# A third exponential tile added on GpSimd in quads 5 to 21 of an attention kernel

## The chip, the cores and the metric

The kernel runs on one NeuronCore of a Trainium2 chip. The metric is the device time of one execution in microseconds, as the median of several runs. TensorE is called PE here, VectorE DVE, ScalarE ACT, GpSimd POOL, and SyncE, which issues most of the DMAs, SP. All data is fp32.

## The reference

The program is an attention with normalised queries and keys, followed by a feed-forward block with the SoLU activation.

```python
# 8 batches, 12 heads, 448 tokens, head size 64
q_n, k_n = rmsnorm(q, g_q), rmsnorm(k, g_k)
scores = q_n @ k_n.T / sqrt(64)
attn = exp(scores - max(scores)); attn = attn / (sum(attn) + 1e-9)
x = (attn @ v), heads side by side             # 3584 tokens x 768
h = x @ w_in                                   # 768 x 1024
solu = h * softmax(h)
y = layernorm(solu) * g_ln @ w_out             # 1024 x 768
```

The part that matters here is the sum of the exponentials over the keys, by which each query's output is divided.

## The kernel before

**Stages.** The attention comes first, then the first product of the feed-forward block (L989), then the second (L1203). Both products are cut into blocks that are combined by sums and differences so that fewer matmuls are needed; POOL makes the combinations of the weights (`combine`, L563). The whole attention lies in one hand-written order of instructions: each engine gets its instructions in the order in which the Python code calls them, and runs them in that order.

**Quads.** The loop at L1383 runs over 24 quads `m`. A quad is four heads, handled as two pairs: `a = 2m` and `b = 2m + 1`. A pair's state is the dictionary `st[n]`, a quad's is `quads[m]`.

**Exponentials.** The 448 keys of a head are three tiles of 128 and a rest of 64. `scores(n, kc)` (L810) multiplies one key tile with all the queries of the pair's two heads into a score tile in PSUM, of which there are three in rotation (`ps_t`, tag `t`), and ACT writes the exponentials to SBUF as `E[n, kc]`, 128 keys by 896 (two heads of 448 queries). The two rests of a quad share one more tile, `E[NJ]` (`scores_last`, L824). No maximum is taken off. The E tiles come from eight rotating buffers.

**Values.** `values_last` and `values` (L852, L865) multiply the tiles with v on PE into the PSUM tiles `o`. Every E tile is read there.

**Sums.** The sum over keys is a sum over partitions, and PE makes it with columns of ones: `sums(m)` (L876) accumulates several terms in the PSUM tile `sm`. Each term is one 128x896 tile and takes four matmuls, each of 224 columns and 32 rows of output (L890). To save terms, DVE first adds the first two tiles of each pair to one, `es` (`add`, L842). Quads 0 to 21 then have five terms: the shared tile of rests, the third tile of a, the third tile of b, es of a and es of b. In the last two quads (`on_vector`, L839) DVE also adds the third tile to es (`add_more`, L847), and there are three terms. Es has two buffers.

**After the sums.** `inverse` (L895) transposes `sm` on DVE (L901), takes the reciprocal (L902) and copies parts of it on POOL (L909). `divide` (L911), called one unit later, spreads the reciprocals (L916) and multiplies (L917); `store_x` (L920) writes the result to DRAM.

**Work for later quads in the same loop.** In quad m the queries and keys of quad m+2 are squared on ACT (`squares`, L662), summed by rows on DVE (`row_sums`, L670), and folded on POOL (`fold_sums`, four copies at L680 and an addition at L681). At the start of the next quad ACT makes the seed of the inverse root from that (L700, L701), DVE refines it (L707 to L710), and POOL multiplies queries and keys by it (`normalise`, L719). DVE transposes the result (`qk_transpose`, L729), ACT applies the gain (`gain`, L733). One raw tile of w_in is converted over two quads in each of quads 4 to 10 and in every second quad after that: two steps on ACT (L535, L536), and in the following quad two joins on DVE (L541, L542).

**Order in a quad from 5 on.** On POOL: `normalise` of a+2 and b+2, combinations of weights in some quads, the fold for quad m+2, the copies of `inverse`. On DVE: the refinement, the division of quad m-1, two transposes, `add(a)`, row sums of a+4 and of b+4, `add(b)`, joins, then `inverse`. On ACT: the seed, seven exponentials, two squares, two gains, conversion steps. On PE: seven score tiles, `values_last` and `values(a)`, `values(b)`, `sums`. The order around the change is at L1482 to L1515:

```python
            unit(lambda: scores(b, 1))
            if early or 1 < m < 4:
                qk_transpose(b + 2)
            if m > 1:
                add(a)
            unit(lambda: scores(b, 2))
            ...
            add_more(a)
            add_more(b)
            unit(outputs)
```

Of the kernel before, what the change touches and what calls it, by code (L numbers as in the profile page):

```python
# [14 lines left out]
OP = AluOpType  # L15
# [351 lines left out]
def fast_path(  # L367
# [24 lines left out]
    nc = tc.nc  # L392
# [225 lines left out]
    st = {}  # L618
# [187 lines left out]
    def exponentials(d, kc, s):  # L806
        d["E", kc] = big_tile("E")[:, 0 : 2 * S].rearrange("p (h t) -> p h t", h=2)
        nc.scalar.activation(d["E", kc], s[:, :, 0:S], AF.Exp)  # L808

    def scores(n, kc):  # L810
        d = st[n]
        s = ps_t.tile([P, 2, 512], FP32, tag="t", name="s")

        for c in range(0, P, D):
            for h in range(2):
                hh = slice(h * D, (h + 1) * D)
                keys = slice(NJ * c + kc, NJ * (c + D - 1) + kc + 1, NJ)
                nc.tensor.matmul(  # L818
                    s[c : c + D, h, 0:S], d["qkT"][hh, 1, keys], d["qkT"][hh, 0, :],
                    start=True, stop=True,  # L820
                )
        exponentials(d, kc, s)
# [16 lines left out]
    def on_vector(m):  # L839
        return m >= NQ - 2  # L840

    def add(n):  # L842
        d = st[n]
        d["es"] = work.tile([P, 2, S], FP32, tag="es", name="es")
        nc.vector.tensor_tensor(d["es"], d["E", 0], d["E", 1], OP.add)  # L845

    def add_more(n):  # L847
        d = st[n]
        if on_vector(n // 2):
            nc.vector.tensor_tensor(d["es"], d["es"], d["E", 2], OP.add)  # L850

    def values_last(m):  # L852

# [22 lines left out]
    def sums(m):  # L876


        d = quads[m]
        sm = d["sm"] = ps_t.tile([P, S // 2], FP32, tag="t", name="sm")  # L880
        terms = [(2, d["E", NJ])]
        for key in ("es",) if on_vector(m) else (2, "es"):
            for i in range(2):
                n = st[2 * m + i]
                terms.append((i, n["E", 2] if key == 2 else n["es"]))
        for x, (w, e) in enumerate(terms):
            for h in range(2):
                for t in range(2):
                    g = 32 * (2 * h + t)
                    nc.tensor.matmul(  # L890
                        sm[g : g + 32, :], ones[:, w], e[:, h, t * S // 2 : (t + 1) * S // 2],
                        start=(x == 0), stop=(x == len(terms) - 1),
                    )
# [421 lines left out]
    def unit(f, steps=4):  # L1315
        nonlocal now
        f()
        now += steps
        due = [x for x in todo if x[0] <= now]
        todo[:] = [x for x in todo if x[0] > now]  # L1320
        for _, g in sorted(due, key=lambda x: x[0]):
            g()
# [40 lines left out]
    with tc.manual_schedule():  # L1363
# [19 lines left out]
        for m in range(NQ):  # L1383
            a, b = 2 * m, 2 * m + 1
# [9 lines left out]
            if m == 0:  # L1394
# [32 lines left out]
                unit(lambda: values(b))  # L1427
                squares(5)
                unit(lambda: sums(m))
                inverse(m)  # L1430
                row_sums(4)
# [52 lines left out]
                qk_transpose(b + 2)  # L1484
            if m > 1:
                add(a)
            unit(lambda: scores(b, 2))
            if m == 1:
                qk_transpose(a + 2)
# [19 lines left out]
                fold_sums(m + 2)  # L1509
            if not scarce:  # L1510
                add(b)
            add_more(a)
            add_more(b)
            unit(outputs)
            step(m - 2)  # L1515
            begin(m)
# [7 lines left out]
            if m == NQ - 1:  # L1524
                block_sums(0, 0)
                block_sums(0, 1)
                load_x(1)
            unit(lambda: sums(m))
            inverse(m)
            if next1 and m not in (1, 2):  # L1530
# [139 lines left out]
@with_exitstack  # L1670
def kernel(
    ctx: ExitStack,
    tc: tile.TileContext,
    q: bass.AP,
    k: bass.AP,
    v: bass.AP,
    g_q: bass.AP,
    g_k: bass.AP,
    moe_w_in: bass.AP,
    moe_w_out: bass.AP,  # L1680
    moe_g_ln: bass.AP,
    out: bass.AP,
):
    nc = tc.nc
    flags = ctx.enter_context(tc.tile_pool(name="flags", bufs=1))
    flag = flags.tile([1, 1], I32, name="flag")
    large = flags.tile([1, 1], FP32, name="large")
    fast_path(tc, q, k, v, moe_w_in, moe_w_out, out, g_q, g_k, moe_g_ln, large)
    nc.vector.tensor_copy(flag, large)
    other = nc.values_load(flag[0:1, 0:1], min_val=0, max_val=1)  # L1690
    with tc.If(other > 0):
        general_path(tc, q, k, v, g_q, g_k, moe_w_in, moe_w_out, moe_g_ln, out)
# [30 lines left out]
```

## Time and profile before

| | |
|---|---|
| median of 3 runs | 816.29 us (816.02 to 816.68) |
| profiled execution | 815.47 us |
| its span | 813.7 us |
| mean granted PE clock | 0.998 of full speed |
| PE busy | 797.9 us |
| DVE busy | 617.0 us |
| ACT busy | 473.9 us |
| POOL busy | 469.0 us |

The attention fills the time to about 325.5 us, where the first matmul of the feed-forward block starts. In a row of the groups, `x` is the number of instructions, then come the busy time in us and the mean of one in ns, then the idle time of the engine just before them and what ended it. In a timeline a row gives the start and the length in us, the engine, the line and the operation, output and input tiles with their shapes, and in brackets the idle time before it and what ended that. Rows with a count stand for several instructions in a row. In a chain a row gives start, length and the line that the end of the span is traced back to. An fp32 matmul leaves two records, so a count of records on PE is twice the number of matmuls.

### The profile page before, as it was taken

To read this page: it belongs to the slowest core of one execution; us is meant where nothing else is said; L and a number is where in the kernel's file an instruction comes from. 1 tells how busy PE (TensorE), PEld (TensorE's weight loads), DVE (VectorE), ACT (ScalarE), POOL (GpSimd) and SP (SyncE) were. 2 spreads that over 40 slices of the span, in tenths; PEclk is the share of its full clock that TensorE was granted. 3 is DMA by queue.
4 is the path that set the end of the run, shared out by engine and by line. 5 is a ranking of instruction groups with operands and counts; after the bars stand their busy time and mean duration, and the time that the engine had idled before them with its cause. 6 is when DMAs were issued, how large, how long until landed. Compare 5 with 4: busy or idle time off the path is not lost.

```text
span 813.7 us, 14586 instructions
## 1 busy us (share of the span) xinstructions
PE 797.9 (98%) x5030; PEld 468.4 (58%) x5030; DVE 617.0 (76%) x1217; ACT 473.9 (58%) x785; POOL 469.0 (58%) x635
## 2 busy tenths in 40 slices
PE   8999999999999999999999999999989999999997
PEld 4334444444444443444444444444679999999996
DVE  6877889888887977478878756777796876866945
ACT  6677878777786865365767545444515454464420
POOL 1353555656555566233356467767497867777761
PEclk9999999999999999999999999999999999999999
DMA  9868798887878644245755344552548457365412
GB/s 165 175 143 157 165 184 185 188 178 159 163 162 180 132 94 123 81 131 142 184 142 146 91 113 122 147 137 64 171 122 279 129 197 245 122 239 181 150 60 83
DMA packets 269600, 122.71 MB, mean 151 GB/s; under 512 B 187596, under 2 KB 254668, under 8 KB 269516
## 3 DMA queue, kind: packets, MB, share of 16 engines
q1 hardware_dynamic: 254332, 111.78, 55.1%
q10 hardware_dynamic: 15184, 9.90, 4.5%
q8 instruction: 42, 0.69, 0.4%
q14 instruction: 42, 0.34, 0.1%
HBM read 84.94 MB, written 36.70 MB: 149 GB/s over the span
## 4 chain that ended last, share of the span: by engine, by line
PE 88%; DVE 5%; POOL 2%; DMA 2%; ACT 2%; issue 1%; SPq 0%; DVEq 0%; POOLq 0%; ACTq 0%
PE A L1203 14%; PE A L989 13%; PE o L871 13%; PE s L818 12%; PE B L989 8%; PE B L1203 7%; PE sm L890 5%; PE C L989 4%; PE D L989 4%; PE C L1203 3%; PE o L860 2%; PE s L831 2%; DMA xg<-xd 1%; ACT E L808 1%; DVE bs L1072 1%
## 5 line engine op out<-in xcount | busy, mean ns | idle before, releaser
L808 ACT ACTIVATE E<-s 128x896 f32<-128x896 f32 x168 | 139.1, 937 | 20.3 <-PE s L818 20.0
L818 PE MATMUL s<-qkT 64*64 64x448 f32 x1152 | 120.5, 545 | 1.4 <-ACT E L808 0.7
L871 PE MATMUL o<-E,v 128*64 128x448 f32 x576 | 113.5, 543 | 0.0
L680 POOL COPY ss<-part 32x56 f32<-32x56 f32 x88 | 42.1, 478 | 91.5 <-DVE part L670 88.8
L719 POOL TENSOR_TENSOR qkn<-qk,ny 128x896 f32<-128x896 f32 x46 | 77.1, 1697 | 21.2 <-DMA qk<-in_k_dram 12.0
L1078 POOL TENSOR_TENSOR he<-he,mhalf 128x1 f32<-128x1 f32 x28 | 27.6, 986 | 105.6 <-DVE he L1077 105.1
L1203 PE MATMUL B<-w_out,sums 128*128 128x192 f32 x392 | 80.0, 327 | 3.3 <-DVE P L1265 2.1
L818 PEld LDWEIGHTS s<-qkT 64*64 64x64 f32 x1152 | 48.1, 163 | 59.6 <-ACT E L808 29.2
L1203 PE MATMUL A<-w_out,sums 128*128 128x192 f32 x392 | 80.0, 327 | 1.2 <-POOL sums L1183 0.8
L871 PEld LDWEIGHTS o<-E,v 128*64 128x64 f32 x576 | 39.2, 137 | 72.7 <-issue 67.3
L989 PE MATMUL B<-w_in,xsum 128*128 128x512 f32 x168 | 76.7, 592 | 0.7 <-POOL he L1078 0.7
L989 PE MATMUL A<-w_in,xg 128*128 128x512 f32 x168 | 74.6, 593 | 0.0
L1060 ACT ACTIVATE u<-h,hmax 128x1024 f32<-128x1024 f32 x28 | 32.2, 1148 | 63.4 <-DVE hmax L1054 63.3
L1203 PEld LDWEIGHTS B<-w_out,sums 128*128 128x128 f32 x392 | 66.1, 190 | 4.0 <-DVE P L1265 2.4
L1203 PEld LDWEIGHTS A<-w_out,sums 128*128 128x128 f32 x392 | 66.1, 190 | 2.1 <-POOL sums L1183 1.3
L989 PEld LDWEIGHTS B<-w_in,xsum 128*128 128x128 f32 x168 | 31.8, 190 | 41.2 <-issue 38.3
L989 PEld LDWEIGHTS A<-w_in,xg 128*128 128x128 f32 x168 | 31.8, 190 | 40.1 <-issue 39.6
L845 DVE TENSOR_TENSOR es<-E 128x896 f32<-128x896 f32 x48 | 53.4, 1114 | 1.3 <-ACT E L808 1.3
L670 DVE TENSOR_REDUCE part<-sq 128x28 f32<-128x896 f32 x46 | 48.1, 1078 | 2.4
L729 DVE STREAM_TRANSPOSE qkT<-qkn 128x896 f32<-128x896 f32 x46 | 48.5, 1088 | 1.8 <-POOL qkn L719 1.8
L1203 PE MATMUL A<-w_out,s 128*128 128x192 f32 x224 | 45.5, 326 | 0.0
L563 POOL TENSOR_TENSOR w_out<-w_out 128x384 f32<-128x384 f32 x44 | 44.5, 1017 | 1.3
(151 smaller groups left out, 1622.4 us busy)
## 6 DMA issues: line engine op xcount, KB each, us to landing
ur<-ud SPq DMA_DIRECT2D x60, 256.0 KB, 4.5
ud<-ub SPq DMA_DIRECT2D x112, 128.0 KB, 2.3
xd<-xo SPq DMA_DIRECT2D x48, 224.0 KB, 3.1
qk<-in_q_dram SPq DMA_DIRECT2D x92, 112.0 KB, 3.1
qk<-in_k_dram SPq DMA_DIRECT2D x92, 112.0 KB, 3.0
v<-in_v_dram SPq DMA_DIRECT2D x24, 384.0 KB, 4.4
out_dram<-P SPq DMA_DIRECT2D x19, 384.0 KB, 3.7
raw<-in_moe_w_in_dram SPq DMA_DIRECT2D x12, 512.0 KB, 4.7
```

Of the source, the lines that this page charges most:

```text
L563: nc.gpsimd.tensor_tensor(o, p, q, OP.subtract)
L670: nc.vector.tensor_reduce(norms[m]["part"][:, i], st[n]["sq"], AX, OP.add)
L680: e.tensor_copy(ss[g * 32 : g * 32 + 32], part[o * 32 : o * 32 + 32])
L719: e.tensor_tensor(d["qkn"].rearrange("p (s b) d -> p s b d", s=2), d["qk"].rearrange("p s (b d) -> p s b d", d=32), y.rearrange("p (s b) - ...
L729: nc.vector.transpose(d["qkT"].rearrange("p s t -> p (s t)"), d["qkn"].rearrange("p b d -> p (b d)"))
L808: nc.scalar.activation(d["E", kc], s[:, :, 0:S], AF.Exp)
L818: nc.tensor.matmul(s[c : c + D, h, 0:S], d["qkT"][hh, 1, keys], d["qkT"][hh, 0, :], start=True, stop=True,)
L845: nc.vector.tensor_tensor(d["es"], d["E", 0], d["E", 1], OP.add)
L871: nc.tensor.matmul(d["o"][h * D : (h + 1) * D, :], quads[n // 2]["v"][:, n % 2 + 2 * h, kc], d["E", kc][:, h], start=False, stop=(kc == NJ ...
L890: nc.tensor.matmul(sm[g : g + 32, :], ones[:, w], e[:, h, t * S // 2 : (t + 1) * S // 2], start=(x == 0), stop=(x == len(terms) - 1),)
L989: nc.tensor.matmul(k[bank], a[:, c], w_in[i][:, c], start=begin and c == 0, stop=c == HD - 1, skip_group_check=not begin,)
L1203: nc.tensor.matmul(k[bank], a[:, c].rearrange("p a i -> p (a i)"), w_out[:, area, i, c], start=begin and c == 0, stop=c == KC - 1, skip_gr ...
```

## The change

In quads 5 to 21 the third tile of pair a is added to its es on POOL, right behind DVE's `add(a)` in the order of the code and ahead of the fold on POOL. The sums of these quads lose the term of that tile and have four terms. The third tile of pair b stays a term of its own. Quads 0 to 4 and the last two are as before; in the last two the two additions of `add_more` stay on DVE at their place.

```diff
+    def whole(n):
+        return on_vector(n // 2) or n > 9 and n % 2 < 1
+
     def add_more(n):
         d = st[n]
-        if on_vector(n // 2):
-            nc.vector.tensor_tensor(d["es"], d["es"], d["E", 2], OP.add)
+        if whole(n):
+            e = nc.vector if on_vector(n // 2) else nc.gpsimd
+            e.tensor_tensor(d["es"], d["es"], d["E", 2], OP.add)
...
         terms = [(2, d["E", NJ])]
-        for key in ("es",) if on_vector(m) else (2, "es"):
+        for key in (2, "es"):
             for i in range(2):
-                n = st[2 * m + i]
-                terms.append((i, n["E", 2] if key == 2 else n["es"]))
+                n = 2 * m + i
+                if key == "es":
+                    terms.append((i, st[n]["es"]))
+                elif not whole(n):
+                    terms.append((i, st[n]["E", 2]))
...
             if m > 1:
                 add(a)
+                if not on_vector(m):
+                    add_more(a)
             unit(lambda: scores(b, 2))
...
-            add_more(a)
-            add_more(b)
+            if on_vector(m):
+                add_more(a)
+                add_more(b)
             unit(outputs)
```

## The prediction

> **What bounds the kernel now.** I read the page first (busy shares, chain), then the chain by time inside the attention stage, then the timeline of each engine in one quad.
>
> ```profile
> span 813.7 us, 14586 instructions
> PE 797.9 (98%) x5030; PEld 468.4 (58%) x5030; DVE 617.0 (76%) x1217; ACT 473.9 (58%) x785; POOL 469.0 (58%) x635
> ```
>
> PE is busy for 98% of the span. The chain that ended last, cut to 95 to 130 us, is PE alone:
>
> ```profile
> 104.85 2.03 PE sm L890 x40
> 106.88 2.45 PE s L818 x24
> 109.33 0.75 PE s L831 x8
> 110.08 2.25 PE s L818 x24
> 112.34 0.75 PE o L860 x8
> 113.09 4.66 PE o L871 x24
> 117.75 2.03 PE sm L890 x40
> 119.78 2.45 PE s L818 x24
> ```
>
> A quad takes 119.78 - 106.88 = 12.90 us, and quads 5 to 21 all start that far apart, so PE sets the pace and the sums are 2.03 us of it. Each matmul has two records: 40 are 20 matmuls, five terms of four. From the timelines of quad 7, in the order POOL, DVE, ACT:
>
> ```profile
> 116.74 2.58 POOL L680 COPY ss<-part 32x56 f32<-32x56 f32 x4 [4.57 <-DVE part L670]
> 119.40 0.30 POOL L681 TENSOR_TENSOR ss<-ss,part 128x56 f32<-128x56 f32 x1
> 113.36 1.05 DVE L845 TENSOR_TENSOR es<-E 128x896 f32<-128x896 f32 x1
> 114.53 2.08 DVE L670 TENSOR_REDUCE part<-sq 128x28 f32<-128x896 f32 x2
> 116.53 1.08 DVE L845 TENSOR_TENSOR es<-E 128x896 f32<-128x896 f32 x1
> 119.84 0.42 DVE L901 STREAM_TRANSPOSE r<-sm 128x224 f32<-128x224 f32 x1 [0.88 <-PE sm L890]
> 119.74 0.34 ACT L700 ACTIVATE ny<-ss,eps 128x56 f32<-128x56 f32 x1 [1.97 <-POOL ss L681]
> 120.12 0.25 ACT L701 ACTIVATE ny<-ny 128x56 f32<-128x56 f32 x1
> 120.79 5.77 ACT L808 ACTIVATE E<-s 128x896 f32<-128x896 f32 x7 [0.42 <-PE s L818]
> ```
>
> What to see: POOL idles 4.57 us before the four copies, DVE waits 0.88 us for the sums, and ACT waits only 0.42 us for the first score tile. That 0.42 us is how far a second loop is from being the bound. This loop runs from seven exponentials through two squares on ACT, two row sums on DVE, the fold on POOL and the inverse root on ACT to the next exponentials. It is 12.90 - 0.42 = 12.48 us, some 12.52 with the 0.04 us by which an engine follows its releaser.
>
> **What the Trainium skill says.** "SBUF — State Buffer", section "Who interferes with whom": a DVE instruction with two SBUF inputs contends with a GpSimd instruction that reads SBUF, the first to issue holds the shared pair for the whole instruction, and a tensor_reduce never contends. The trace agrees. The four copies take 1.02 us where DVE runs neither an add nor a weight join, 1.75 beside the add es, and 2.58 beside it and the joins of L541 and L542:
>
> ```profile
> 79.05 1.02 POOL L680 COPY ss<-part 32x56 f32<-32x56 f32 x4 [5.57 <-DVE part L670]
> 181.22 1.75 POOL L680 COPY ss<-part 32x56 f32<-32x56 f32 x4 [4.56 <-DVE part L670]
> ```
>
> "Perfetto Trace Analysis", section "Optimizing Scalar/DVE Operations", warns that moving work between DVE and GpSimd might not help because of this port; here the work moves from PE, but the port still matters. Of the third page I use a price, below.
>
> **The change part by part.**
>
> *Removed from PE.* One term in each of quads 5 to 21, four matmuls (8 records). A quad with five terms spends 2.03 us in the sums. Quad 23, which already has three, spends 1.27 (324.26 to 325.53 in the chain). So a term is (2.03 - 1.27) / 2 = 0.38 us, and 17 x 0.38 = 6.46 us of PE time goes. The period PE asks for becomes 12.52 us.
>
> *Added on POOL.* 17 additions of 128x896 with two full inputs, written in place. No row shows it. Nearest rows:
>
> ```profile
> L563 POOL TENSOR_TENSOR w_out<-w_out 128x384 f32<-128x384 f32 x44 | 44.5, 1017 | 1.3
> L563 POOL TENSOR_TENSOR w_in<-w_in,w_in x12: 1272/1280/2045, 137.9 to 315.9; 128x512 f32<-128x512 f32 x12
> ```
>
> From 384 to 512 elements is 263 ns, 2.05 ns each, so 1280 + 384 x 2.05 = 2068 ns. "GPSIMD Engine Reference", section 3.1, gives 4497 ns for 2048 elements; scaled to 896 that is an estimate of 1967 plus some fixed cost, in agreement. Lower bound: the same-sized multiply of L719, 1697 ns, whose second input is a broadcast. Upper bound: 834 ns for 256 elements (L1181) without a fixed part, 2919 ns. I take 2.07 us.
>
> *When it runs.* It waits for es of a, which ends at 114.41 in quad 7. POOL follows DVE by 0.13 us (part ends 116.61, copies start 116.74), so it runs from 114.54 to 116.61, inside the 4.57 us of idleness. Beside it DVE runs the two row sums, which read one input and don't block it. Next on POOL are the fold's copies, held by part until 116.74; with the 0.08 us between POOL instructions they could start at 116.69. They aren't late. If the cover were gone, 2.07 us would go into the second loop each time.
>
> *The port.* DVE issues es of b at 116.53, with 0.08 us of the POOL addition left, and is blocked until 116.61. A blocked add finishes sooner after its release than its full duration: the one issued at 319.43 took 1.56 us but ended 0.95 after L970 let go at 320.04. So es of b ends near 117.6 as now, and joins and copies behind it keep their places. I put 0 to 0.1 us here.
>
> *The added waits.* Behind the waiting addition on POOL stands only the fold; ACT's inverse root waits for that. The combination of weights (L563, quads 9 to 21 in part) is ahead of it and ends before es of a does (139.21 against 140.19 in quad 9). PE now waits for POOL in the es term of a, which it reaches about 118.5, 1.9 us after the addition. Es has two buffers, as before, and E of a's third tile is still read by the values product, so no buffer is held longer. No DMA is added or moved; SP's queue is unchanged.
>
> *The second loop.* 12.52 us in the twelve quads with a weight join (5 to 11, 13, 15, 17, 19, 21), against PE's new 12.52: level. In the other five it has 2.58 - 1.75 = 0.83 us to spare, which also takes up what the quad before was late. PE feels lateness of ACT only when it lacks a score buffer, after about 0.1 to 0.2 us. So only the run of quads 5 to 11 can pile it up. At 0.05 us a quad that is 0.35 less about 0.15, so 0.2 us.
>
> *After quad 21* the stall at load xg (landing 312.65, ACT then late for quad 23) hangs on sums of 21 through divide and store, so it moves with them: 0.05 us for its own waits.
>
> Sum: 6.46 - 0.2 - 0.05 = 6.2 us. The profiled execution was 815.47 us (span 813.7, 1.8 around it); it becomes 809.3, span 807.5. The median of the runs is 816.29, 0.8 above that execution; minus 6.2 it is 810.1.
>
> **The rivals.**
>
> *Partly eaten by the second loop (811.9).* The addition takes 2.3 us, or the port's handover costs 0.2 to 0.3 us, so the twelve join quads are late by x = 0.25 us. Quads 5 to 11 lose 7 x 0.25 = 1.75; 13 to 21 lose 5 x (0.25 - 0.2) = 0.25, since each is followed by a quad with room. Gain 6.4 - 2.0 = 4.4 us. For it: the loop is level with PE to 0.05 us. Against it: the fit of 2.07, and a DVE that blocks nothing before es of b. Its spread, x from 0.1 to 0.4, is a gain of 5.6 to 2.5.
>
> *All of it eaten (816).* x near 0.6: 7 x 0.6 + 5 x 0.4 = 6.2, nothing left. This needs an addition of some 2.7 us, or copies that lose the port once more to a join (0.7 us).
>
> *Slower (818.5).* The GpSimd addition is the bound: at the upper price of 2.92 us it ends 0.80 us after the copies should start, and es of b, joins, copies and inverse root all follow it. Join quads 5 to 11 then take 12.52 + 0.80 = 13.32 us, 0.42 more than now, together +3.0. Quads 12 to 21 gain 10 x 0.38 = 3.8 and lose 5 x 0.6 = 3.0. Net +2.2 us. It decides from about 2.7 us on (x = 0.62 is break-even). Against it: only the short 256-element rows are that dear per element.
>
> That the change doesn't do what it says can't be: the removed term is in the instruction count, 136 fewer PE records.
>
> **How the numbers follow.** Full gain (5.6 to 6.5 us) 0.62; partly eaten (2.5 to 5.6) 0.22; eaten to within 0.2% (1.6 us, what a measurement of this kernel can tell from no change) 0.08; slower 0.08. PE caps the gain at 6.5 us, so the low end, with spread of the median, is 809.2; leaving out eaten and slower, the high end is 813.8. Faster 0.84, same 0.08, slower 0.08.
>
> **What would show it.** Sums at 1.65 us a quad with 32 records; starts of quads 5 to 21 12.52 us apart; a GpSimd row of 17 at about 2.07 us; ACT's wait for the first score tile down from 0.42 to near 0 in join quads; POOL's idle time before the copies from 4.57 to about 2.2, and copies still 2.58 and 1.75. Wrong if join quads are over 12.7 us apart, if es of b gets longer than 1.3 us, or if PE waits for ACT in the scores.

## The result and the profile after

The changed kernel takes 809.82 us (median of 4 runs, 809.46 to 811.44) against 816.15 us before. The ratio is 0.9928, with a 95% interval of 0.9911 to 0.9945. A later series of the same kernel, `after_again` below, gave 809.00 us and 0.9918 (0.9904 to 0.9932). The prediction was 810.1 us, between 809.2 and 813.8, and 807.5 us for the span of the profiled execution, which is 807.7 us. The later series lies just under the low end.

The first lines of the page of the changed kernel:

```profile
span 807.7 us, 14348 instructions
PE 793.2 (98%) x4894; PEld 466.1 (58%) x4894; DVE 615.4 (76%) x1217; ACT 474.0 (59%) x785; POOL 505.7 (63%) x652
```

PE has 136 records fewer (17 terms of 8), POOL has 17 instructions more and 36.7 us more work, and DVE and ACT have as many instructions as before. In the chain of the changed kernel the sums of quads 5 and 6 stand at:

```profile
87.43 4.66 PE o L875 x24
92.09 1.65 PE sm L897 x32
...
99.95 4.66 PE o L875 x24
104.61 1.65 PE sm L897 x32
```

The sums are 1.65 us long in place of 2.03, and the quads are 104.61 - 92.09 = 12.52 us apart in place of 12.90. The timelines of quad 7 of the changed kernel, in the order POOL, DVE, ACT:

```profile
113.93 2.11 POOL L854 TENSOR_TENSOR es<-es,E 128x896 f32<-128x896 f32 x1 [2.37 <-ACT sq L662]
116.12 2.58 POOL L680 COPY ss<-part 32x56 f32<-32x56 f32 x4
112.74 1.05 DVE L845 TENSOR_TENSOR es<-E 128x896 f32<-128x896 f32 x1
113.91 2.08 DVE L670 TENSOR_REDUCE part<-sq 128x28 f32<-128x896 f32 x2
115.91 1.08 DVE L845 TENSOR_TENSOR es<-E 128x896 f32<-128x896 f32 x1
118.84 0.42 DVE L908 STREAM_TRANSPOSE r<-sm 128x224 f32<-128x224 f32 x1 [0.49 <-PE sm L897]
119.50 0.25 ACT L701 ACTIVATE ny<-ny 128x56 f32<-128x56 f32 x1
119.79 5.77 ACT L808 ACTIVATE E<-s 128x896 f32<-128x896 f32 x7
```

The addition starts 0.14 us after es of a ends (113.79) and ends at 116.04. (The bracket names ACT's square, which ends at about the same time. By the order of the code the addition needs es and nothing of the square.) The fold's copies start at 116.12, 0.13 us after the row sums end at 115.99, the same distance as in the kernel before, so they start no later than the row sums let them. They also follow the addition by 0.08 us, the distance between two instructions on POOL seen before (119.32 to 119.40), so the addition fits with nothing to spare. Es of b takes 1.08 us as before, and the copies 2.58. DVE's wait for the sums is down from 0.88 to 0.49 us, and ACT no longer shows a wait at the first exponential.

Where the 6.0 us of the span came from, from the starts of `values_last` on PE (L860 before, L864 after) and the first matmul of the feed-forward block:

| | before | after | gain |
|---|---|---|---|
| quads 5 to 21, each | 12.89 to 12.90 us | 12.51 to 12.52 us | 17 x 0.379 = 6.44 |
| quad 22 to 23 | 13.06 us | 12.29 us | 0.77 |
| start of the kernel to quad 1 | 32.19 us | 32.32 us | -0.13 |
| all that follows the attention | 488.24 us | 489.31 us | -1.07 |

The first row is the change. The other three weren't expected. The start of quad 1 lies between 32.03 and 32.41 us in the ten traces of this case, so its 0.13 us is within what varies from one to another; the last section says more of the other two.

### The profile page after: what moved, and what is told of

It is laid out like the page before. It is cut to its first block, busy times and chain, and to the rows that moved or that the text cites. A ratio compares the mean times of both kernels' runs of the same rounds, so it can differ in the third digit from the quotient of the medians.

```text
span 807.7 us, 14348 instructions
## 1 busy us (share of the span) xinstructions
PE 793.2 (98%) x4894; PEld 466.1 (58%) x4894; DVE 615.4 (76%) x1217; ACT 474.0 (59%) x785; POOL 505.7 (63%) x652
## 4 chain that ended last, share of the span: by engine, by line
PE 91%; DVE 4%; ACT 1%; DMA 1%; POOL 1%; issue 1%; SPq 0%; DVEq 0%; POOLq 0%; ACTq 0%
PE A L1210 15%; PE o L875 13%; PE s L818 13%; PE A L996 13%; PE B L996 8%; PE B L1210 7%; PE sm L897 5%; PE C L996 4%; PE D L996 4%; PE C L1210 4%; PE o L864 2%; PE s L831 2%; DMA ur<-ud 1%; ACT E L808 1%; DVE ub L1100 1%
## 5 line engine op out<-in xcount | busy, mean ns | idle before, releaser
L854 POOL TENSOR_TENSOR es<-es,E 128x896 f32<-128x896 f32 x17 | 35.9, 2110 | 30.4 <-ACT sq L662 30.4
```

Source lines behind the costliest of these rows:

```text
L854: e.tensor_tensor(d["es"], d["es"], d["E", 2], OP.add)
```

## Experiments

Each experiment below starts from the changed kernel. The third column gives the distances of quads 5 to 11 (all with weight joins on DVE), the fourth those of the five quads without joins (12, 14, 16, 18, 20), and the last two the end of the attention and the rest of the span in the profiled execution.

| kernel | us, ratio to before | 5 to 11 | no joins | attention ends | rest |
|---|---|---|---|---|---|
| before | 816.15 | 12.90 | 12.90 | 325.46 | 488.24 |
| changed | 809.82, 0.9928 | 12.52 | 12.52 | 318.39 | 489.31 |
| after_again | 809.00, 0.9918 (0.9904 to 0.9932) | 12.52 | 12.52 | 318.17 | 489.03 |
| terms_only | 808.94, 0.9907 (0.9894 to 0.9921) | 12.52 | 12.52 | 318.08 | 488.92 |
| add_only | 815.71, 0.9995 (0.9987 to 1.0003) | 12.90 | 12.90 | 325.43 | 489.27 |
| longer | 815.64, 0.9995 (0.9988 to 1.0001) | 13.06 to 13.14 | 12.52 to 12.59 | 325.46 | 488.24 |
| three_terms | 805.00, 0.9857 (0.9842 to 0.9872) | 12.33 to 12.39 | 12.14 | 314.79 | 489.21 |
| bare_terms | 805.29, 0.9872 (0.9857 to 0.9887) | 12.32 to 12.36 | 12.14 | 314.50 | 488.30 |
| vector_a | 818.26, 1.0022 (1.0014 to 1.0031) | 13.08 to 13.12 | 12.81 | 327.56 | 489.24 |
| more_adds | 809.97, 0.9923 (0.9909 to 0.9937) | 12.52 | 12.49 to 12.50 | 319.97 | 488.23 |

### The two halves of the change

`terms_only` drops the GpSimd additions and keeps the shorter sums:

```diff
-                if not on_vector(m):
-                    add_more(a)
```

> The changed kernel without its 17 GpSimd additions: the third tile of a is left out of the sums of quads 5 to 21, so PE has four terms there and POOL the work of before. Theory (the addition lies wholly in POOL's idle time): join quads stay 12.52 us apart and the time is that of the changed kernel, 809 to 811 us. Rival (the addition costs through the port or the fold, 0.1 us or more in each of the twelve join quads): at least 1.2 us under the changed kernel, below 808.6 us.

`add_only` keeps all five terms and writes the addition aside:

```diff
-            e = nc.vector if on_vector(n // 2) else nc.gpsimd
-            e.tensor_tensor(d["es"], d["es"], d["E", 2], OP.add)
+            if on_vector(n // 2):
+                nc.vector.tensor_tensor(d["es"], d["es"], d["E", 2], OP.add)
+            else:
+                aside = work.tile([P, 2, S], FP32, tag="aside", name="aside", bufs=1)
+                nc.gpsimd.tensor_tensor(aside, d["es"], d["E", 2], OP.add)
...
-                elif not whole(n):
+                elif not on_vector(m):
```

> The 17 additions alone: POOL writes them to a tile of their own that nobody reads, and PE keeps five terms. Theory: quads 5 to 21 stay 12.90 us apart, since the loop of exponentials, row sums and fold has 0.38 us more room here than in the changed kernel; 816 us, as before. Rival (GpSimd reads slow DVE or the fold by more than that room): over 817.5 us, quads over 12.95 us apart.

The shorter sums alone give 12.52 us a quad, as with the additions. The additions alone leave 12.90, and the time isn't told from before. The first median was 0.9 us over that of `terms_only`, so I ran the changed kernel again:

> The changed kernel once more. If the 0.9 us between it and the run without the additions (809.8 and 808.9) is only spread between chips and executions, its median comes out within 0.5 us of 809, and quads 5 to 21 are 12.52 us apart. If the additions cost something, it stays at 809.8 or more.

It came out at 809.00, 0.06 us from `terms_only`. So the gain in quads 5 to 21 is PE's removed work, and the additions cost nothing that these runs can tell.

### How long the second loop is

`three_terms` takes another term from PE without putting anything in its place, so that PE no longer sets the pace. `bare_terms` is the same without the additions.

```diff
-                elif not whole(n):
+                elif m < 5:
```

> The changed kernel with the third tile of b also left out of the sums of quads 5 to 21, and nothing in its place: PE has three terms and asks for 12.14 us a quad. Theory (second loop of 12.5 us in join quads): quads 5 to 11 stay 12.4 to 12.5 us apart, only the five quads without joins get shorter, at most 5 x 0.38 = 1.9 us in all: 807.5 to 809.5 us, and ACT no longer waits for PE at the first exponential of a join quad. Rival (PE the only bound): 17 x 0.38 = 6.5 us, so 803.4 us, quads 12.14 us apart.

> Three terms in quads 5 to 21 and no GpSimd addition: the third tiles of a and b are left out of the sums. Theory (the addition ends just when the row sums let the fold start, so the second loop is the same without it): join quads 12.32 to 12.39 us apart as with it, others 12.14, 804 to 805.5 us. Rival (the addition holds up the fold): join quads come down towards 12.2 us, 803 to 804 us.

The quads without joins follow PE to 12.14 us. The join quads (those with weight joins on DVE) stop at 12.32 to 12.39 us, so there is a second loop and it binds there. But it is about 0.15 us shorter than the 12.48 to 12.52 us of the prediction, and the time fell to 805.0 us, below the 807.5 that I had set as the lowest. With and without the addition the join quads are the same to 0.04 us, so the addition doesn't lengthen the loop; without it the fold's copies still wait for the row sums (4.49 us idle before them in quad 7 of `bare_terms`). ACT's timeline of `bare_terms`, where the loop binds, shows what was misread:

```profile
107.06 5.75 ACT L808 ACTIVATE E<-s 128x896 f32<-128x896 f32 x7
...
119.25 0.25 ACT L701 ACTIVATE ny<-ny 128x56 f32<-128x56 f32 x1
119.41 1.70 ACT L808 ACTIVATE E<-s 128x896 f32<-128x896 f32 x2
```

The exponential starts 0.16 us after the start of the row before it, although that row is 0.25 us long: rows of ACT overlap here. The distance is 0.15 or 0.16 us in all twelve join quads of this kernel. In the kernel before the two starts were 120.79 - 120.12 = 0.67 us apart, so the room was 0.67 - 0.16 = 0.51 us and not the 0.42 us of the bracket, and the loop 12.90 - 0.51 = 12.39 us. Against PE's 12.52 us it leaves about 0.13 us. The changed kernel shows the same room: there the two starts are 0.29 us apart (119.50 and 119.79 above), 0.13 us more than 0.16.

### A longer GpSimd work: the rival that ends slower

```diff
             e = nc.vector if on_vector(n // 2) else nc.gpsimd
+            if e is nc.gpsimd:
+                aside = work.tile([P, S // 2], FP32, tag="aside", name="aside", bufs=1)
+                e.tensor_tensor(aside, d["es"][:, 0, 0 : S // 2], d["E", 2][:, 0, 0 : S // 2], OP.add)
```

> The changed kernel with a further GpSimd addition of 128x224 into a tile that nobody reads, just ahead of each of the 17. From 1280 ns for 512 elements and 2.05 ns for each element less it takes 0.69 us, with the gap 0.77. Theory (the second loop is level with PE in join quads): quads 5 to 11 are 13.2 to 13.3 us apart, quads 12 to 21 in pairs of some 25.5 us, and the gain is gone: 6.5 - 7 x 0.77 - 5 x 0.57 = -1.75, so 815 to 818.5 us. Rival (PE alone sets the pace and buffers take up the lateness): 12.52 us apart, 810 us.

POOL and DVE in quad 7 of this kernel:

```profile
115.13 0.66 POOL L856 TENSOR_TENSOR aside<-es,E 128x224 f32<-128x224 f32 x1 [2.26 <-ACT sq L662]
115.87 2.11 POOL L857 TENSOR_TENSOR es<-es,E 128x896 f32<-128x896 f32 x1
118.05 2.60 POOL L680 COPY ss<-part 32x56 f32<-32x56 f32 x4
117.15 1.78 DVE L845 TENSOR_TENSOR es<-E 128x896 f32<-128x896 f32 x1
```

The extra work is 115.87 - 115.13 = 0.74 us. Es of b, issued at 117.15 while POOL still reads, grows from 1.08 to 1.78 us and ends 0.95 us after POOL's 117.98. The copies, which the row sums would have let start near 117.4, stand behind it all. The join quads go to 13.06 to 13.14 us, which is 12.36 + 0.74 = 13.10, and the gain is gone: 815.64 us, not told from before. The join quads are shorter than the 13.2 to 13.3 us expected, by the room in the loop. So the mechanism of the slower rival is real. The whole of its 0.56 us over PE's pace reached PE in each join quad, and the quads without joins took up nothing of it, against my 0.1 to 0.2 us of slack at the score buffers. The room that there is lies in the loop itself.

### The same addition on DVE

`vector_a` makes the 17 additions on DVE, behind es of b:

```diff
-            e = nc.vector if on_vector(n // 2) else nc.gpsimd
-            e.tensor_tensor(d["es"], d["es"], d["E", 2], OP.add)
+            nc.vector.tensor_tensor(d["es"], d["es"], d["E", 2], OP.add)
...
-                if not on_vector(m):
-                    add_more(a)
...
+            add_more(a)
             if on_vector(m):
-                add_more(a)
                 add_more(b)
```

> The changed kernel with the 17 additions on DVE behind es of b, ahead of the joins, in place of GpSimd. Theory: in join quads the fold's copies are blocked by one more DVE addition, 0.7 to 0.8 us, so the second loop is 12.36 + 0.75 = 13.1 us there, and DVE has only 0.49 us of waiting left to give for 1.0 us of work; the other quads stay at 12.52. Total like the kernel with the longer GpSimd work: 815 to 817 us. Rival (any engine with idle time will do): 809.5 us.

It is slower than before. POOL and then PE in quad 7 of this kernel:

```profile
117.24 3.35 POOL L680 COPY ss<-part 32x56 f32<-32x56 f32 x4 [4.49 <-DVE part L670]
118.14 0.96 PE L896 MATMUL sm<-E,ones 128*32 128x224 f32 x16
119.19 0.96 PE L896 MATMUL sm<-es,ones 128*32 128x224 f32 x16
```

One more DVE instruction with two SBUF inputs beside the copies makes them 3.35 us in place of 2.58, and the join quads 13.08 to 13.12 us, as expected. What I missed is the order of the sums. The es terms start 1.05 us after the E terms, against 0.78 us in the changed kernel (293.08 - 292.30 in its quad 21). PE waits some 0.27 us for the late es of a, in quad 12, which has no joins, too (184.78 - 183.73), and the quads without joins stand at 12.81 in place of 12.52. That is 5 x 0.29 = 1.5 us, enough for the 1.26 us by which the time lies above the 817 that I had allowed.

### More terms taken from PE

`more_adds` adds the third tile of a on GpSimd in quad 4 too, and the third tile of b on DVE in the five quads without joins:

```diff
+    def spare(m):
+        return 4 < m < NQ - 2 and m - 1 not in steps_at
+
     def whole(n):
-        return on_vector(n // 2) or n > 9 and n % 2 < 1
+        return on_vector(n // 2) or n > 7 and n % 2 < 1 or n % 2 > 0 and spare(n // 2)
...
-            e = nc.vector if on_vector(n // 2) else nc.gpsimd
+            e = nc.vector if on_vector(n // 2) or n % 2 else nc.gpsimd
...
             if on_vector(m):
                 add_more(a)
+            if on_vector(m) or spare(m):
                 add_more(b)
```

> The changed kernel with six more terms replaced by additions: that of a in quad 4 on GpSimd, and that of b in quads 12, 14, 16, 18 and 20 on DVE behind es of b. Those five have no weight joins; the fold's copies get one more DVE addition beside them (1.75 to about 2.58 us), so their second loop becomes the 12.36 us of the join quads, above the 12.14 us of PE. Theory (loop of 12.36 us): quad 4 gains 0.38 us, the five are 12.36 us apart for a gain of 5 x 0.16, in all 1.2 us under the changed kernel. Rival (only PE counts): 6 x 0.38 = 2.3 us under it. Second rival (es of b comes too late for the sums, which it reaches some 0.8 us into them): no gain.

No gain over the changed kernel (809.97 against 809.00 in the same series), as the second rival has it. PE's sums in quad 12 of this kernel:

```profile
179.61 0.56 PE L900 MATMUL sm<-es,ones 128*32 128x224 f32 x8
180.32 0.59 PE L900 MATMUL sm<-es,ones 128*32 128x224 f32 x8 [0.15 <-DVE es L857]
```

The last term starts 0.71 us after the one before it, where 0.38 us is the pace of a term. PE saves a term and waits 0.33 us for b's sum, so these quads are 12.49 to 12.50 us apart. Quad 4 came down from 12.90 to 12.75 us only, and not to 12.52. In quad 4 the order on DVE is another: es of b stands between the two row sums. Here it is issued while the GpSimd addition reads:

```profile
75.70 2.11 POOL L857 TENSOR_TENSOR es<-es,E 128x896 f32<-128x896 f32 x1 [2.37 <-ACT sq L662]
76.69 2.08 DVE L845 TENSOR_TENSOR es<-E 128x896 f32<-128x896 f32 x1
```

It takes 2.08 us in place of 1.08 and ends 0.96 us after the addition's 77.81. The second row sum and the fold behind it are late by that microsecond, and the next exponential follows the inverse root on ACT by 0.16 us (81.69 to 81.85), the distance at which the second loop binds. So the same addition that costs nothing from quad 5 on costs 0.23 us in quad 4. In this execution the load of xg was also the slowest of all, as the last section tells.

## Why the prediction was right

- **Removed term, 0.38 us.** Measured 0.379 a quad, 6.44 us in all.
- **Addition, 2.07 us from rows of other sizes.** Measured 2.104 to 2.116:

```profile
L854 POOL TENSOR_TENSOR es<-es,E x17: 2104/2110/2116, 88.9 to 289.2; 128x896 f32<-128x896 f32 x17
```

- **Its place.** It fits between es of a and the end of the row sums, and the copies start with the row sums. `bare_terms` shows that nothing of it enters the loop.
- **The port.** The 0 to 0.1 us held for es of b (1.08 us as before), and the two row sums took 2.08 us beside the addition as they did without it. `longer` shows what lies behind that edge: 0.74 us more, and all the gain is lost.
- **The second loop.** Here a term of the sum was mis-sized: 12.32 to 12.39 us in place of 12.52, so the 0.2 us that quads 5 to 11 were to pile up was nothing. The idle bracket had been taken for the whole room.
- **The slower rival.** Its place was right, and its price a little high: it put break-even at 0.62 us of delay. In `longer` 0.74 us made quads 5 to 21 0.5 us longer in all than before, 0.04 us for each of the twelve join quads, so break-even lies at about 0.70 us by this estimate. The loop had room that the prediction didn't count, and the slack at the score buffers that it did count was not there.
- **After quad 21.** Wrong: "moves with them, 0.05 us". The stall between quads 22 and 23 shrank by 0.77 us.
- **The rest of the kernel.** It was taken as unchanged and was 1.07 us longer in that execution, in which PE's clock fell for a stretch (last section).
- **The cap.** The low end of 809.2 us rested on PE's 6.5 us as the most that could be gained. The second series gained 7.2 us, 816.20 to 809.00. Quads 5 to 21 gave no more than before, so the excess lies outside them.

Against the sum of the prediction these are +0.2 us for the loop, +0.82 for quads 22 and 23 (0.77 gained in place of 0.05 lost), -1.07 for the rest and -0.13 for the start of the kernel. They cancel to -0.18 us, so that 807.5 us against 807.7 us is luck in part. What carries the result is the first four.

## What to carry to other kernels

When work is taken from the engine that sets the pace, ask which loop through the other engines comes next, and measure its length by starts and not by idle brackets. The work given to GpSimd was free here because it lay in a gap where DVE ran single-input instructions and nothing behind it on GpSimd was due yet; the gap was 2.3 us (113.79 to 116.12) for an instruction of 2.1, and 0.74 us more cost the whole gain. The engine with idle time isn't enough: the same addition on DVE, which waits 0.49 to 1.9 us a quad, made the kernel slower.

## What was not expected of the hardware

**PE's clock in the last stage.** What follows the attention took 488.2 to 488.3 us in four of the ten profiled executions and 488.9 to 489.3 in the six others. The difference lies some 15 us behind the start of the second product. There PE first waits 2.15 us for DVE. Two stretches of 5 us, before and behind the end of that wait, in the kernel before and then in the changed one; the first busy time is PE's, and the third number from the end is the granted clock:

```profile
588.60:593.60 5.00, 2.86 (x16) 2.56 (x16) 4.83 (x13) 3.54 (x6) 4.59 (x8) 1.00 0.66 219
593.60:598.60 5.00, 4.99 (x30) 4.79 (x31) 4.25 (x9) 0.07 (x1) 4.92 (x8) 1.00 0.73 206
```

```profile
581.28:586.28 5.00, 2.86 (x17) 2.56 (x17) 4.83 (x13) 3.54 (x6) 4.58 (x8) 1.00 0.66 223
586.28:591.28 5.00, 5.00 (x20) 5.00 (x21) 2.86 (x8) 0.30 (x2) 4.92 (x8) 0.66 0.77 210
```

In the changed kernel the clock is down to 0.66 for the 5 us behind the wait, and PE, though busy all the time, gets through 20 records in place of 30. All ten traces have this wait, of 2.14 or 2.15 us. The clock falls behind it in six of them (changed, `after_again`, `terms_only`, `add_only`, `three_terms`, `vector_a`) and in four not (before, `longer`, `bare_terms`, `more_adds`). `add_only` has the fall at the pace of the kernel before, and `more_adds` doesn't have it at a pace near that of the changed one, so neither the change nor the wait alone decides it. What does is open.

By its mean granted clock one kernel shows both. The mean of the ten profiled executions is 0.998 where the clock doesn't fall and 0.996 or 0.997 where it does. In the 16 runs of the kernel before that go with `after_again`, the eight at 0.998 or more took 815.3 to 816.0 us and the eight at 0.997 or less 816.4 to 817.6. The four runs of the changed kernel in the first series all had 0.996, those of `after_again` 0.996 to 0.998. Some of the 0.8 us between these two medians may come from there. In the traces the fall goes with 0.6 to 1.1 us of an execution, up to a sixth of what was measured here.

**The load of xg.** It took, from issue to landing, 4.9 us in `terms_only`, 5.1 in `after_again`, 5.6 in `longer`, 5.7 in the changed kernel, 5.8 in `bare_terms`, 6.2 in `three_terms`, 6.4 in `add_only`, 6.5 before and in `vector_a`, and 7.8 in `more_adds`. Quads 22 and 23 are 12.26, 12.26, 12.32, 12.29, 12.36, 12.70, 13.02, 13.06, 13.06 and 14.34 us apart in the same order. So beyond some 5.8 us each further microsecond of the load is about one more between the two quads, and the 0.77 us in the table agree with the 0.8 us between 6.5 and 5.7. In the kernel before the chain that ended last runs through the load, in the changed one it doesn't:

```profile
306.18 6.46 DMA xg<-xd
```

Why the same transfer takes longer in one trace than in another stays open, and so does whether that goes with the kernel or with the execution: each kernel has one trace, and no run here was made to tell it.
